# Gated mix of cached attention and a ReLU layer: part of w1 loaded as a separate 96-row transfer, VectorE and ScalarE in loops over one unit

## The chip, the cores and the metric

The kernel runs on one core of a Trainium2 chip. The metric is the device time of one execution in microseconds, as the median of several runs. The core has five engines with queues of their own: PE (TensorE, matmuls), DVE (VectorE), ACT (ScalarE), POOL (GpSimd) and SP (SyncE, which here issues every DMA). They meet only through semaphores. Sixteen DMA engines carry what SP issues.

## The reference

Batch is 2 with one token each (decode), D is 448, there are 16 heads of 256 and 4096 cached positions, and Dff is 1792. All arrays are float32.

```python
g = sigmoid((x * gate_w).sum(-1, keepdims=True))
q = (x @ wq), as 16 heads of 256
p = softmax(q . k_cache * 256**-0.5)          # over 4096 positions, for each of 2 x 16 heads
a = (p . v_cache), heads side by side, @ wo
b = relu(x @ w1) @ w2
out = g * a + (1 - g) * b
```

The caches are 268 MB of the 289.5 MB that are read.

## The kernel before, in words

**Units.** The work of the caches is cut into U = 32 units, one for each pair of batch and head. A unit's k and v are one block of 128 partitions x 16,384 floats (8.39 MB): the first half is k, the second v. Three such blocks fit in SBUF, slot[0] to slot[2]; unit u lies in slot (u + 1) mod 3. The first transfer, wq (with x and the gate's weights as its last 12 columns), takes slot[0]; kv[0] and kv[1] follow in slots 1 and 2.

**SP** (L170 to L192) issues all transfers in one queue. It refills a slot when the semaphore freed says that the unit in it is done: kv[u + 3] after unit u. The last unit's k and v halves come as two transfers (L181, L182), the second with a semaphore last_v of its own. Behind them, when unit 29 is done, come w1 and w2 into slot[0] (L184, L185), and, when unit 30 is done, wo into slot[1] in six pieces of 14, 8, 4, 3, 2 and 1 blocks of 448 columns (L189). The result goes out at L192.

**The start.** DVE spreads x over several columns (xr, xn and xl, L344 to L348), and PE computes the gate (L206) and q in two halves (project, L103 to L114; the transposes of q at L221). ACT copies them to SBUF (L309, L311).

**A unit** takes four steps. PE multiplies k with the query (L129, 16 matmuls that write sc in PSUM) and sets scored. DVE takes the negative maximum (L143) and sets maxed. ACT makes p = exp(sc + nm) with its sum (L136), sets raised, and copies the next unit's query to qc (L138, queried). DVE multiplies v with p in eight instructions that each sum up one column of ov (L149), and sets freed. PE can begin the next unit's scores as soon as the exp is through. DVE and ACT run ten passes of a loop over three units (L357, L316) and then two more units written out (L322, L363), with fixed addresses. PE loops over three units (L223).

**The tail.** PE starts the hidden layer h = x @ w1 when w1 has landed (L241, hidden). The 1792 columns are four groups of 448, one for each 32-row strip g of PSUM; the 448 rows of w1 are contracted in blocks of 128, 128, 128 and 64, the last of which holds two groups side by side in 128 partitions (L112). When freed reaches 32, PE transposes the maxima and sums (L244, L245), DVE and ACT work out the weights of the softmax's parts (L367 to L373), DVE scales ov into os (L375), and oc spreads the result (L378). ACT makes the ReLU (L326) and hr (L328, L331); PE multiplies hr with w2 (L267), and then oc with each piece of wo as it lands: 26 blocks into acc (L279), copied out by DVE (L382), and folded together with the last six blocks straight into z (L287, L292). DVE copies z to res (L384), and SP sends it out.

Of the kernel before, what the change touches and what calls it, by code (L numbers as in the profile page):

```python
# [3 lines left out]
F32 = mybir.dt.float32  # L4
# [14 lines left out]
def gated_mix_decode(nc, wq, kv, wm, wo, out):  # L19
# [11 lines left out]
    NW = wq.shape[1] - KC * (B + 1)  # L31
    FG = 448
    NF = 14
    W1 = 2 * (2 * KF * FG + FG)
# [15 lines left out]
    slot = [nc.alloc_sbuf_tensor_at(f"slot{i}", [P, SW], F32, offset=first + i * SW * 4).ap() for i in range(SLOTS)]  # L50
# [13 lines left out]
    scored, maxed, raised, queried, freed = (ev() for _ in range(5))  # L64
# [11 lines left out]
    xn = sb("xn", P, P // B, B)  # L76
    ge = sb("ge", P, 1)
# [3 lines left out]
    qt = sb("qt", P, U, T)  # L81
# [3 lines left out]
    ov = sb("ov", P, U, J)  # L85
    p = sb("p", P, SG)
# [29 lines left out]
    xg = slot[0][:, NW:wq.shape[1]].rearrange("p (c b) -> p c b", c=KC)  # L116

    ident_0, ident_ok, par_ok, xl_0 = ev(), ev(), ev(), ev()
# [15 lines left out]
    def unit_act(u, u_wait, s, s_next, last=False):  # L134
        act.wait_ge(maxed, u_wait)
        act.activation(p, sc, AF.Exp, bias=nm[:, bass.ds(u, 1)], accum_out=ls[:, bass.ds(u, 1)]).then_inc(raised, 1)  # L136
        if not last:
            act.activation(qc[:, s_next, :], qt[:, bass.ds(u + 1, 1), :].rearrange("p o t -> p (o t)"),  # L138
                           AF.Copy).then_inc(queried, 1)

    def unit_dve(u, u_wait, s, v_sem=None):
        dve.wait_ge(scored, u_wait)
        dve.tensor_reduce(nm[:, bass.ds(u, 1)], sc, axis=AX.X, op=ALU.max, negate=True).then_inc(maxed, 1)  # L143
        dve.wait_ge(raised, u_wait)
        if v_sem is not None:
            dve.wait_ge(v_sem, 16)
        for j in range(J):
            v = slot[s][:, SW // 2 + j * SG:SW // 2 + (j + 1) * SG]
            m = dve.scalar_tensor_tensor(v, v, 1.0, p, op0=ALU.mult, op1=ALU.mult,  # L149
                                         accum_out=ov[:, bass.ds(u, 1), j].rearrange("p o -> p o"))  # L150
        m.then_inc(freed, 1)
# [4 lines left out]
    U1 = (LOOP - 1) * SLOTS  # L156

# [4 lines left out]
    w2 = slot[0][:, W1:W1 + NF * D]  # L162
    w_o = slot[1]

    with nc.Block(no_gpsimd_drain=True) as block:

        @block.sync
        def _(_e):
# [15 lines left out]
            sp.dma_start(w1, wm[:, :W1]).then_inc(w1_in, 16)  # L184
            sp.dma_start(w2, wm[:, W1:]).then_inc(w2_in, 16)  # L185
# [49 lines left out]
        def pe_tail():  # L235
            half = W1 // 2
            def hidden(lo, hi):
                return project(pa, w1, lambda c, g: g // 2 * half + (g % 2 * KF + c) * FG,
                               lambda i: i * half + 2 * KF * FG, FG, lo, hi)

            pe.wait_ge(w1_in, 16)  # L241
# [8 lines left out]
            hidden(KF, KC).then_inc(hid_mm, 1)  # L250
            pe.wait_ge(os_ok, 1)
# [52 lines left out]
        def _(_e):  # L304
            act.wait_ge(gate_mm, 1)
# [139 lines left out]
```

## Time and profile before

| what | value |
|---|---|
| time, median of 3 runs | 676.09 us (675.98 to 676.59) |
| the profiled execution | 675.9 us |
| its span, first to last instruction | 674.5 us |
| read from HBM | 289.54 MB, 429 GB/s over the span |
| busy | PE 215.3 us, DVE 340.9 us, ACT 46.4 us, POOL 0.8 us |
| granted TensorE clock, mean | 0.674 |

The span is 1.4 us shorter than the execution's own time. Times in the views count from the span's start. The busy shares add up over the span and say nothing of what waits for what. A timeline row has its start, its length, the engine, the line, what was written and read, and in brackets the idle time before it with what ended it. A row of the windows view has the stretch, its length, each engine's busy time with the number of instructions, the granted clock, the mean busy share of the 16 DMA engines, and GB/s. A DMA share below 1 means that some of the sixteen have nothing to carry.

### The profile page before, as it was taken

What the parts mean: (1) busy time and instruction counts of PE and PEld (TensorE: products, weight loads), DVE (VectorE), ACT (ScalarE), POOL (GpSimd) and SP (SyncE); (2) the same over time, 40 slices, a digit from 0 to 9 for tenths busy, and PEclk for the clock granted to TensorE, in tenths of its full rate; (3) what the DMA queues carried; (4) which work ended last, traced back from release to release, by engine and by line L of the source; (5) the groups of instructions that cost most, each with busy time, mean ns of one, the idle gap of its engine ahead of it and who ended that gap; (6) DMA issues with size and microseconds to landing.
All of it is one profiled execution on the core that took longest, in us unless ns stands there. A gap on an engine that the chain in (4) does not pass through costs nothing.

```text
span 674.5 us, 3929 instructions
## 1 busy us (share of the span) xinstructions
PE 215.3 (32%) x1279; PEld 52.6 (8%) x1279; DVE 340.9 (51%) x566; ACT 46.4 (7%) x107; POOL 0.8 (0%) x7
## 2 busy tenths in 40 slices
PE   0643212333232213323321233333212333332456
PEld 0210000000000000000000000000000000000012
DVE  0015566554555665454556645446566544556670
ACT  0010000000000000000000000000000000000110
POOL 0000000000000000000000000000000000000000
PEclk9976566676756677676556767765676776655878
DMA  9999999999999999999999999999999999999997
GB/s 381 428 435 436 436 435 435 435 435 435 435 435 435 435 435 435 435 435 431 435 435 435 435 435 435 435 435 435 435 435 435 435 435 431 435 435 408 432 431 301
DMA packets 6084, 289.61 MB, mean 429 GB/s; under 512 B 704, under 2 KB 832, under 8 KB 1216
## 3 DMA queue, kind: packets, MB, share of 16 engines
q1 hardware_dynamic: 6080, 289.55, 99.2%
q8 instruction: 3, 0.05, 0.0%
q14 instruction: 1, 0.01, 0.0%
HBM read 289.54 MB, written 0.01 MB: 429 GB/s over the span
## 4 chain that ended last, share of the span: by engine, by line
DMA 68%; DVE 13%; PE 12%; issue 6%; ACT 1%; DVEq 1%; SPq 0%; ACTq 0%
DMA slot<-in_kv 64%; DVE slot L149 11%; PE sc L129 10%; DMA slot<-in_wo 3%; DVE nm L143 2%; PE acc L279 1%; ACT p L136 1%; DVEq L149 1%; PE z L292 0%; SPq L176 0%; DVE a_sb L382 0%; DVEq L143 0%; ACTq L136 0%; PE z L287 0%; SPq L66 0%
## 5 line engine op out<-in xcount | busy, mean ns | idle before, releaser
L149 DVE SCALAR_TENSOR_TENSOR slot<-slot,p 128x1024 f32<-128x1024 f32 x256 | 295.9, 1222 | 47.1 <-ACT p L136 47.1
L129 PE MATMUL sc<-slot,qc 128*32 128x512 f32 x1024 | 182.9, 880 | 415.9 <-DMA slot<-in_kv 415.9
L143 DVE TENSOR_REDUCE nm<-sc 128x1024 f32 (+1 forms) x32 | 39.2, 1225 | 243.7 <-PE sc L129 243.7
L129 PEld LDWEIGHTS sc<-slot,qc 128*32 128x32 f32 x1024 | 41.3, 154 | 556.9 <-issue 552.6
L136 ACT ACTIVATE p<-sc,nm 128x1024 f32<-128x1024 f32 x32 | 35.7, 1114 | 562.9 <-DVE nm L143 562.9
L149 DVE DVE_READ_ACCUMULATOR slot<-slot,p (+1 forms) x256 | 21.5, 84 | 0.0
L344 DVE COPY xr<-slot 128x384 f32<-128x384 f32 x1 | 0.6, 553 | 18.1 <-DMA slot<-in_wq 18.1
L206 PE MATMUL pa<-slot,xr 128*128 128x1 f32 x6 | 1.4, 355 | 21.4 <-DVE xl L348 21.4
L279 PE MATMUL acc<-slot,oc 128*32 128x448 f32 x52 | 7.2, 672 | 3.2 <-DMA slot<-in_wo 3.2
L109 PE MATMUL pb<-slot,xr 128*32 128x512 f32 x48 | 8.1, 829 | 0.0
L382 DVE COPY a_sb<-acc 128x448 f32<-128x448 f32 x1 | 0.6, 625 | 14.6 <-PE acc L279 14.6
L109 PE MATMUL pa<-slot,xr 128*32 128x448 f32 x24 | 4.0, 793 | 12.1 <-DMA slot<-in_wm 12.1
L136 ACT ACTIVATION_READ_ACCUMULATOR p<-sc,nm (+1 forms) x32 | 6.2, 193 | 0.0
L138 ACT ACTIVATE qc<-qt 128x2 f32 (+1 forms) x31 | 6.0, 192 | 0.0
L267 PE MATMUL acc<-slot,hr 128*32 128x448 f32 x28 | 3.2, 541 | 1.0 <-ACT hr L331 1.0
L206 PEld LDWEIGHTS pa<-slot,xr 128*128 128x128 f32 x6 | 1.4, 325 | 21.4 <-DVE xl L348 21.4
L279 PEld LDWEIGHTS acc<-slot,oc 128*32 128x32 f32 x52 | 2.3, 126 | 8.2 <-issue 6.9
L112 PE MATMUL pb<-slot,xl 128*64 128x512 f32 x8 | 2.2, 618 | 0.0
L109 PEld LDWEIGHTS pb<-slot,xr 128*32 128x32 f32 x48 | 1.7, 137 | 4.0 <-issue 4.0
L109 PEld LDWEIGHTS pa<-slot,xr 128*32 128x32 f32 x24 | 0.8, 141 | 14.3 <-DMA slot<-in_wm 13.0
L309 ACT ACTIVATE q<-pb 128x512 f32<-128x512 f32 x2 | 1.2, 597 | 9.7 <-PE pb L112 9.7
L378 DVE COPY oc<-pc 128x256 f32<-128x256 f32 x4 | 1.4, 418 | 0.8 <-PE pc L254 0.8
(54 smaller groups left out, 21.0 us busy)
## 6 DMA issues: line engine op xcount, KB each, us to landing
slot<-in_kv SPq DMA_DIRECT2D x2, 4096.0 KB, 35.4
slot<-in_wq SPq DMA_DIRECT2D x1, 7174.0 KB, 19.6
slot<-in_wm SPq DMA_DIRECT2D x2, 3136.0 KB, 31.5
slot<-in_wo SPq DMA_DIRECT2D x1, 3136.0 KB, 23.6
slot<-in_wo SPq DMA_DIRECT2D x1, 1792.0 KB, 27.5
slot<-in_wo SPq DMA_DIRECT2D x1, 896.0 KB, 29.1
slot<-in_wo SPq DMA_DIRECT2D x1, 672.0 KB, 30.3
slot<-in_kv SPq DMA_DIRECT2D x31, 39.9
```

Source lines behind the costliest of these rows:

```text
L109: m = pe.matmul(dst[g * R:(g + 1) * R, :n], x_of(c), w[:, at(c, g):at(c, g) + n], start=(c == 0), stop=False)
L112: m = pe.matmul(dst[i * HP:(i + 1) * HP, :n], xl.rearrange("p j r b -> p (j r b)"), w[:, at_last(i):at_last(i) + n], start=False, stop=True)
L129: m = pe.matmul(sc[g * R:(g + 1) * R, c * CW:(c + 1) * CW], qc[:, s, t:t + 1].to_broadcast([P, R]), slot[s][:, lo:lo + CW], start=(t == 0) ...
L136: act.activation(p, sc, AF.Exp, bias=nm[:, bass.ds(u, 1)], accum_out=ls[:, bass.ds(u, 1)]).then_inc(raised, 1)
L138: act.activation(qc[:, s_next, :], qt[:, bass.ds(u + 1, 1), :].rearrange("p o t -> p (o t)"), AF.Copy).then_inc(queried, 1)
L143: dve.tensor_reduce(nm[:, bass.ds(u, 1)], sc, axis=AX.X, op=ALU.max, negate=True).then_inc(maxed, 1)
L149: m = dve.scalar_tensor_tensor(v, v, 1.0, p, op0=ALU.mult, op1=ALU.mult, accum_out=ov[:, bass.ds(u, 1), j].rearrange("p o -> p o"))
L206: m = pe.matmul(pa[:, :1], x_of(c, P) if c < KF else xn[r].rearrange("p r b -> p (r b)"), xg[r, c, B:], start=(c == 0), stop=(c == KC - 1))
L267: pe.matmul(acc[g * R:(g + 1) * R, :D], hr[:, k, :], w2[:, k * D:(k + 1) * D], start=(k < G), stop=False)
L279: m = pe.matmul(acc[g * R:(g + 1) * R, :D], o_of(k), w_o[:, k * D:(k + 1) * D], start=False, stop=(k >= n - G))
L309: act.activation(q, pb, AF.Copy, scale=SCALE).then_inc(q_ok, 1)
L378: m = dve.tensor_copy(oc[:, h], pc[:, h * B * J:(h + 1) * B * J].rearrange("p (o b j) -> p j o b", o=1, b=B) .to_broadcast([P, J, RB, B]))
```

## The change

**w1.** Two of the four groups of columns are contracted as before, in blocks of 128, 128, 128 and 64 rows. The other two are contracted in blocks of 128, 128, 96 and 96 rows. Their first two blocks stay in the array wm; the two of 96 rows form a new array, we, of 12 groups of 9 rows, of which the ninth is not used. SP loads w1's main part (128 x 4928), then we's 96 x 1792, then w2. PE waits for both parts of w1 (w1_in at 32), and has one matmul more. A third layout of x, xe, holds the 96 rows of x; it comes as three more columns of wq's array.

**Loops.** DVE and ACT run all 32 units in loops of one unit, with addresses computed from the loop's register; the three slots are one tensor, ring. DVE sums into a small tile on, which ACT copies to ov after each unit (waiting for freed). ACT copies a query in every pass, so that qt has a 33rd entry, which GpSimd sets to zero. DVE waits in every pass for last_v at 1, which GpSimd sets, and in the last at 17.

**Moved.** xr, xn, xl (and xe) are made by ACT, fold by GpSimd; PE waits for fold_ok ahead of L254's step.

```diff
-    W1 = 2 * (2 * KF * FG + FG)
+    PS = 96
+    W1 = 2 * KF * FG + FG + 4 * FG
+    WE = 4 * FG
...
-    slot = [nc.alloc_sbuf_tensor_at(f"slot{i}", [P, SW], F32, offset=first + i * SW * 4).ap() for i in range(SLOTS)]
+    ring = nc.alloc_sbuf_tensor_at("ring", [P, SLOTS * SW], F32, offset=first).ap()
+    slot = [ring[:, i * SW:(i + 1) * SW] for i in range(SLOTS)]
...
-    w2 = slot[0][:, W1:W1 + NF * D]
+    w1e = slot[0][:PS, W1:W1 + WE]
+    w2 = slot[0][:, W1 + WE:W1 + WE + NF * D]
...
             sp.dma_start(w1, wm[:, :W1]).then_inc(w1_in, 16)
+            sp.dma_start(w1e, we[:, :8]).then_inc(w1_in, 16)
             sp.dma_start(w2, wm[:, W1:]).then_inc(w2_in, 16)
...
+            pool.memset(qt[:, U, :], 0.0).then_inc(last_v, 1)
+            pool.wait_ge(par_ok, 1)
+            pool.tensor_scalar(fold, par[:, None, :].to_broadcast([P, RB, B]), 1.0 / RB, None, op0=ALU.mult
+                               ).then_inc(fold_ok, 1)
...
-            half = W1 // 2
+            half = 2 * KF * FG + FG
+
             def hidden(lo, hi):
-                return project(pa, w1, lambda c, g: g // 2 * half + (g % 2 * KF + c) * FG,
-                               lambda i: i * half + 2 * KF * FG, FG, lo, hi)
-
-            pe.wait_ge(w1_in, 16)
+                for c in range(lo, hi):
+                    for g in range(G):
+                        i, h = divmod(g, 2)
+                        if i == 0 and c == KF:
+                            if g == 0:
+                                pe.matmul(pa[:HP, :FG], xl.rearrange("p j r b -> p (j r b)"),
+                                          w1[:, 2 * KF * FG:half], start=False, stop=True)
+                            continue
+                        x, at = x_of(c) if c < KF else xe.rearrange("p r b -> p (r b)"), (h * KF + c) * FG
+                        if i:
+                            at = half + (h * 2 + c) * FG if c < 2 else (h * 2 + c - 2) * FG
+                        w = w1e if i and c >= 2 else w1
+                        m = pe.matmul(pa[g * R:(g + 1) * R, :FG], x[:PS] if w is w1e else x, w[:, at:at + FG],
+                                      start=(c == 0), stop=(c == KC - 1))
+                return m
+
+            pe.wait_ge(w1_in, 32)
...
+            pe.wait_ge(fold_ok, 1)
             pe.wait_ge(os_ok, 1)
...
+            act.wait_ge(slot_in[0], 16)
+            act.activation(xr, xg[:, :KF, None, :B].to_broadcast([P, KF, P // B, B]), AF.Copy)
+            act.activation(xn, xg[:, KF:KC, :B].to_broadcast([P, P // B, B]), AF.Copy)
+            act.activation(xe, xg[:, KC:, :B].to_broadcast([P, RB, B]), AF.Copy)
...
-            with nc.Fori(0, LOOP - 1, engines=(ET.Activation,)) as r:
-                u0 = act.snap(r * SLOTS)
-                for k in range(SLOTS):
-                    u = act.snap(u0 + k)
-                    unit_act(u, u + 1, (k + 1) % SLOTS, (k + 2) % SLOTS)
-            for u in range(U1, U):
-                unit_act(u, u + 1, (u + 1) % SLOTS, (u + 2) % SLOTS, u == U - 1)
+            qf = qc.rearrange("p s t -> p (s t)")
+            with nc.Fori(0, U, engines=(ET.Activation,)) as u:
+                act.wait_ge(maxed, u + 1)
+                act.activation(p, sc, AF.Exp, bias=nm[:, bass.ds(u, 1)], accum_out=ls[:, bass.ds(u, 1)]
+                               ).then_inc(raised, 1)
+                act.activation(qf[:, bass.ds((u + 2) % SLOTS * T, T)],
+                               qt[:, bass.ds(u + 1, 1), :].rearrange("p o t -> p (o t)"), AF.Copy).then_inc(queried, 1)
+                act.wait_ge(freed, u + 1)
+                act.activation(ov[:, bass.ds(u, 1), :].rearrange("p o j -> p (o j)"), on, AF.Copy).then_inc(kept, 1)
...
-            with nc.Fori(0, LOOP - 1, engines=(ET.DVE,)) as r:
-                u0 = dve.snap(r * SLOTS)
-                for k in range(SLOTS):
-                    u = dve.snap(u0 + k)
-                    unit_dve(u, u + 1, (k + 1) % SLOTS)
-            for u in range(U1, U):
-                unit_dve(u, u + 1, (u + 1) % SLOTS, last_v if u == U - 1 else None)
+            with nc.Fori(0, U, engines=(ET.DVE,)) as u:
+                v0 = dve.snap((u + 1) % SLOTS * SW)
+                dve.wait_ge(scored, u + 1)
+                dve.tensor_reduce(nm[:, bass.ds(u, 1)], sc, axis=AX.X, op=ALU.max, negate=True).then_inc(maxed, 1)
+                dve.wait_ge(raised, u + 1)
+                dve.wait_ge(last_v, (u + 1) // U * 16 + 1)
+                for j in range(J):
+                    v = ring[:, bass.ds(v0 + (SW // 2 + j * SG), SG)]
+                    m = dve.scalar_tensor_tensor(v, v, 1.0, p, op0=ALU.mult, op1=ALU.mult, accum_out=on[:, j:j + 1])
+                m.then_inc(freed, 1)
...
+    rest = w1[2 * P:, 1].reshape(2, PS, 2, FG).transpose(1, 2, 0, 3).reshape(PS // 8, 8, -1)
+    we = np.zeros((PS // 8, 9, rest.shape[2]), np.float32)
+    we[:, :8] = rest
+    w1 = np.concatenate([full, last, both], 1)
```

More of the change, by code (lines that the diff above doesn't have):

```diff
@@ L16, with gated_mix_decode @@
 DIRECT = (3, 2, 1)
-def gated_mix_decode(nc, wq, kv, wm, wo, out):
+def gated_mix_decode(nc, wq, kv, wm, we, wo, out):
     U, _, SW = kv.shape
@@ L63, in gated_mix_decode @@
     wo_in = [ev() for _ in ACC + DIRECT]
-    scored, maxed, raised, queried, freed = (ev() for _ in range(5))
+    scored, maxed, raised, queried, freed, kept = (ev() for _ in range(6))
     sp.dma_start(slot[0][:, :wq.shape[1]], wq).then_inc(slot_in[0], 16)
@@ L114, in project @@
         return m
-    xg = slot[0][:, NW:wq.shape[1]].rearrange("p (c b) -> p c b", c=KC)
-    ident_0, ident_ok, par_ok, xl_0 = ev(), ev(), ev(), ev()
+    xg = slot[0][:, NW:wq.shape[1]].rearrange("p (c b) -> p c b", c=KC + 1)
+    ident_0, ident_ok, par_ok, fold_ok, xl_0 = (ev() for _ in range(5))
     x_ok, gate_mm, gate_ok, ge_ok, gp_ok, omg_ok = (ev() for _ in range(6))
@@ L132, in unit_pe, with oc_of @@
         m.then_inc(scored, 1)
[L134 to L151, printed above, removed]
+    def oc_of(h):
+        return (pc[:, h * B * J:(h + 1) * B * J].rearrange("p (o b j) -> p j o b", o=1, b=B)
+                .to_broadcast([P, J, RB, B]))
     LOOP = -(-U // SLOTS)
     FULL = U - (LOOP - 1) * SLOTS
-    U1 = (LOOP - 1) * SLOTS
+    assert U == 32
     hid_mm, hid_ok, hid_tr, hr_ok = ev(), ev(), ev(), ev()
```

40 lines of the change are left out of this document (20 added, 20 removed).

## The prediction

> **What bounds the kernel now.** I read the page's queues and its chain first, then the windows view (busy time, granted clock and DMA share by stretch), then the timeline of both ends, and last the single lines that the change touches. From the page, the span, the queues (packets, MB, share of 16 engines) and the chain:
>
> ```profile
> span 674.5 us, 3929 instructions
> q1 hardware_dynamic: 6080, 289.55, 99.2%
> q8 instruction: 3, 0.05, 0.0%
> q14 instruction: 1, 0.01, 0.0%
> DMA 68%; DVE 13%; PE 12%; issue 6%; ACT 1%; DVEq 1%; SPq 0%; ACTq 0%
> ```
>
> The SP queue keeps the 16 DMA engines at work for 99.2% of the span, so bytes set the time. DVE and PE stand in the chain only because the view walks back through the wait for a free slot. The next rows show this, and how the transfers run out (the last two columns are the DMA share and GB/s):
>
> ```profile
> 100.00:600.00 500.00, 147.27 (x828) 33.06 (x820) 272.45 (x442) 33.73 (x78) 0.00 (x0) 0.64 1.00 434
> 669.60:671.40 1.80, 1.16 (x40) 0.93 (x44) 0.59 (x1) 0.00 (x0) 0.00 (x0) 1.00 0.27 106
> ```
>
> ```profile
> 669.60:669.80 0.20, 0.00 (x0) 0.00 (x0) 0.20 (x1) 0.00 (x0) 0.00 (x0) 1.00 0.86 332
> 669.80:670.00 0.20, 0.00 (x0) 0.00 (x0) 0.20 (x1) 0.00 (x0) 0.00 (x0) 1.00 0.52 197
> 670.00:670.20 0.20, 0.00 (x0) 0.00 (x0) 0.19 (x1) 0.00 (x0) 0.00 (x0) 1.00 0.28 108
> 670.20:670.40 0.20, 0.16 (x8) 0.16 (x12) 0.00 (x0) 0.00 (x0) 0.00 (x0) 1.00 0.20 81
> 670.40:670.60 0.20, 0.20 (x16) 0.20 (x12) 0.00 (x0) 0.00 (x0) 0.00 (x0) 1.00 0.18 72
> 670.60:670.80 0.20, 0.20 (x20) 0.20 (x12) 0.00 (x0) 0.00 (x0) 0.00 (x0) 1.00 0.12 45
> 670.80:671.00 0.20, 0.20 (x20) 0.17 (x8) 0.00 (x0) 0.00 (x0) 0.00 (x0) 1.00 0.14 54
> 671.00:671.20 0.20, 0.20 (x12) 0.00 (x1) 0.00 (x0) 0.00 (x0) 0.00 (x0) 1.00 0.12 45
> 671.20:671.40 0.20, 0.20 (x11) 0.20 (x12) 0.00 (x0) 0.00 (x0) 0.00 (x0) 1.00 0.05 18
> ```
>
> Over 500 us the share is 1.00 at 434 GB/s, 27.1 GB/s an engine. At the end the engines do not stop together. A share of 0.28 is 4.5 engines, 0.20 three, 0.12 two, 0.05 one. So about twelve have no more to do by 670.2, one more stops about 670.4, one about 670.6, and the last two about 671.3. The row of 1.8 us holds 0.27 x 1.8 = 0.49 us of work an engine: had all stopped together, it would have been at 670.1, some 1.2 us earlier. That is all that a better spread of bytes can win here.
>
> The timeline shows that the last landing sets the end:
>
> ```profile
> 655.87 3.20 PE L267 MATMUL acc<-slot,hr 128*32 128x448 f32 x28 [1.01 <-ACT hr L331]
> ...
> 662.25 7.25 PE L279 MATMUL acc<-slot,oc 128*32 128x448 f32 x52 [3.18 <-DMA slot<-in_wo]
> ...
> 672.51 0.59 SPq L192 DMA_DIRECT2D out<-res  x1
> ```
>
> PE has done everything else by 659.07 and then stands 3.18 us for the first piece of wo. From there each piece is used as it lands, and 3.2 us after the last (671.3 to 674.5) the span ends. So the tail's arithmetic has 3.2 us to spare, and the last engine's last byte has none.
>
> **The transfer in two pieces.** This is the term that decides. The DMA issues (KB each, us to landing) and the pieces in the program's order on SP, before and then after, from the last half of v to the first piece of wo:
>
> ```profile
> slot<-in_wm SPq DMA_DIRECT2D x2, 3136.0 KB, 31.5
> ...
> slot<-in_kv SPq DMA_DIRECT2D x31, 39.9
> ```
>
> ```order
> L182 DMA slot_51<-in_kv 128x8192
> L184 DMA slot_49<-in_wm 128x6272
> L185 DMA slot_49<-in_wm 128x6272
> L189 DMA slot_50<-in_wo 128x6272
> L189 DMA slot_50<-in_wo 128x3584
> ```
>
> ```order
> L172 DMA ring<-in_kv 128x8192
> L174 DMA ring<-in_wm 128x4928
> L175 DMA ring<-in_we 96x1x1792
> L176 DMA ring<-in_wm 128x6272
> L180 DMA ring<-in_wo 128x6272
> L180 DMA ring<-in_wo 128x3584
> ```
>
> The bytes stay: 128 x 4928 + 96 x 1792 elements are the 128 x 6272 of before. The new transfer is 688 KB, and its source has three levels (12 groups of 8 rows, a ninth row skipped), which before has nowhere. If it is spread over all 16 engines, each carries 43.0 KB of it and the term is nothing. If by its 12 groups, twelve engines carry 57.3 KB, 14.3 KB more: 14.3 / 27.1 = 0.53 us later; the other four carry none: 43.0 / 27.1 = 1.59 us earlier. Everything behind it on the queue (w2, wo) shifts engine by engine by as much. I take the twelve, since nothing but the skipped row stands between this source and a plain block of 96 rows. [...] No row here shows a transfer of that kind.
>
> What that is worth depends on which four. If they hold the last two engines and the third latest, those now stop by 671.3 - 1.59 = 669.7, and the end goes to the fourth latest (about 670.3) or the bulk's end (670.15), plus 0.53: 670.7 to 670.85. That is 0.45 to 0.6 us before 671.3; I take **-0.5 us**. If one of the last two is among the twelve, the end is 671.3 + 0.53: **+0.5 us**.
>
> **The loops.** DVE after the last pass and the turn of its loop, before (the last two units written out) and after (all 32 in the loop; ISA rows compute register addresses):
>
> ```order
> L149 SCALAR_TENSOR_TENSOR slot_49,ov<-slot_49,p 128x1024
> L357 REGISTER_ALU
> L357 COMPARE_AND_BRANCH
> L143 TENSOR_REDUCE nm<-sc 128x1
> L149 SCALAR_TENSOR_TENSOR slot_50,ov<-slot_50,p 128x1024 x8
> L143 TENSOR_REDUCE nm<-sc 128x1
> L149 SCALAR_TENSOR_TENSOR slot_51,ov<-slot_51,p 128x1024 x8
> L367 TENSOR_REDUCE nb<-pc 32x1
> ```
>
> ```order
> L376 ISA
> L376 SCALAR_TENSOR_TENSOR ring,on<-ring,p 128x1024
> L368 REGISTER_ALU
> L368 COMPARE_AND_BRANCH
> L381 TENSOR_REDUCE nb<-pc 32x1
> ```
>
> So units 30 and 31 now pay register work, a branch lies between them, and one lies ahead of nb. Their prices, from the line views (ns min/median/max) and the timeline, the first product in the loop (unit 29) and written out (unit 30), with DVE's idle time before it in brackets:
>
> ```profile
> L357 DVEq COMPARE_BRANCH  x10: 50/56/67, 90.3 to 612.2; - x10
> ```
>
> ```profile
> 609.67 1.23 DVE L149 SCALAR_TENSOR_TENSOR slot<-slot,p 128x1024 f32<-128x1024 f32 x1 [1.48 <-ACT p L136]
> ...
> 629.25 1.23 DVE L149 SCALAR_TENSOR_TENSOR slot<-slot,p 128x1024 f32<-128x1024 f32 x1 [1.27 <-ACT p L136]
> ```
>
> In the loop DVE stands 1.48 us between reduce and first product, while ACT makes the exp; written out it stands 1.27: 0.2 us for the register work of both engines. With one ISA more for the wait on the last v, and one ahead of the reduce, I take 0.3 us a unit, 0.6 for two, and 0.2 for two turns of the loop. ACT now waits for freed behind each exp, then copies on into ov; queued behind it is the next exp, which cannot start before DVE's reduce. The copy is like that of qc:
>
> ```profile
> L138 ACT ACTIVATE qc<-qt x31: 191/192/194, 49.0 to 629.1; 128x2 f32 x30, 128x2 f32<-128x2 f32 x1
> ```
>
> Its 0.2 us lie beside the reduce of 1.2 us: nothing. The projection has one matmul more:
>
> ```profile
> 652.23 0.97 PE L112 MATMUL pa<-slot,xl 128*64 128x448 f32 x4
> ```
>
> Two matmuls of four passes took 0.97 us, so +0.5. PE's wait for w1_in now covers both pieces, so that its first half may start 0.53 us late; it has to be through when DVE frees unit 31:
>
> ```profile
> 647.01 3.05 PE L109 MATMUL pa<-slot,xr 128*32 128x448 f32 x16 [12.09 <-DMA slot<-in_wm]
> ...
> 650.23 0.28 PE L244 MATMUL pc<-ident,nm 128*32 128x128 f32 x1 [0.17 <-DVE slot L149]
> ```
>
> It ended at 650.06, so that 0.4 us would show, if DVE did not itself come 0.8 us later (above): nothing more. Sum on the tail's arithmetic: 0.6 + 0.2 + 0.5 = 1.3 us, under the 3.18 us for which PE waits for wo (2.7 if wo comes 0.5 earlier). Nothing shows; without that cover it would be +1.3. In the 30 units before, freed comes 0.3 us later; a slot's transfer takes 39.9 us from issue to landing, of which 8.39 MB at 434 GB/s are 19.3, so 20 us of queue hide it. [...]
>
> **The start.** xr, xn and xl go from DVE to ACT, with xe added, and fold to GpSimd, which is idle until then:
>
> ```profile
> 20.41 0.55 DVE L344 COPY xr<-slot 128x384 f32<-128x384 f32 x1 [18.13 <-DMA slot<-in_wq]
> ...
> 29.70 0.60 ACT L309 ACTIVATE q<-pb 128x512 f32<-128x512 f32 x1 [6.13 <-PE pb L112]
> ...
> 36.35 0.20 ACT L315 ACTIVATE qc<-qt 128x2 f32<-128x2 f32 x1
> ...
> 39.83 6.48 PE L129 MATMUL sc<-slot,qc 128*32 128x512 f32 x32 [3.75 <-DMA slot<-in_kv]
> ```
>
> ACT copies 512 columns in 0.60 us, DVE 384 in 0.55: about the same, plus 0.2 for xe and some 0.2 for a fixed cost in each. The query is ready at 36.55, PE then waits until 39.83 for kv[0], so 0.4 us is hidden. wq grows from 57,392 to 57,404 bytes a row, no longer a multiple of 16; nothing before has such a row. At the same rate it is 1.5 KB in all, nothing; at half rate 17 us. I take nothing.
>
> **The sum.** 674.5 - 0.5 = 674.0 us of span; the profiled execution took 675.9, so 675.4. The median of the runs is 676.09: **675.6 us**.
>
> **The rivals.** About 0.2%, 1.35 us, can be told from no change.
> 1. *A late engine is among the twelve* (0.36): +0.5, 676.6 us. For it: nothing in the page says which engines are late; four drawn at random would hold both of the last two once in twenty. Against: the late ones are about four, apart from a bulk of twelve, and the page has four instruction fetches in the span, whose packets run on these engines, which would single out the same few. [...]
> 2. *The small transfer runs on 8 engines or fewer* (0.06): on 8 each carries 86.0 KB, 1.59 us more. With a late one among them the end is 677.7 us, slower by 0.24%; 9 engines would be 1.2 us, so 8 is where it decides. For it: no transfer of before has such a source. Against: 12 divides into it evenly.
> 3. *The tail's arithmetic comes late* (0.04): if a turn of the loop cost 2 us more than the branch row says, twice on the path, 1.3 + 4.0 - 2.7 = +2.6, 678.2 us. The 67 ns speak against it.
> 4. *wq's row slows its transfer* (0.03): up to +17 us.
> 5. *Nothing moves* (0.06): the transfer is spread over all 16: 676.1 us.
>
> **How the numbers follow.** The forecast has 0.45. It and the fifth are within 0.2%; so is the first, its scatter (the runs span 0.6 us) aside. Levelling wins at most 1.2 us, so faster by over 0.2% needs that scatter: 0.06. Slower: 0.09, from the second (where a late one is in it), third and fourth, and the first's edge. Same: 0.85. The range: 0.7 below the forecast for the most of levelling, and up to 677.0 for the first with its scatter.
>
> **What would show it.** In the windows after: a share that stays near 0.75 for about 1 us or less before the end (four engines done), then falls quickly, is the forecast; a share of 0.05 to 0.12 lasting until 671.8 is the first rival. w2's and wo's landings, PE's wait ahead of the first acc<-wo matmul (above 1 us, or the third rival), and the first use of wq (at 20.41 before) show the rest. A change of over 1.35 us either way would make it wrong.

## The result, and the profile after

| | before | after |
|---|---|---|
| median | 676.08 us (675.86 to 677.01, 6 runs) | 680.25 us (678.6 to 681.19, 6 runs) |
| ratio of the runs | | 1.0054, 95% interval 1.0043 to 1.0065 |
| profiled execution, its span | 675.9 us, 674.5 us | 678.6 us, 676.3 us |

The changed kernel is slower by 0.54%, and the forecast's range (674.9 to 677.0) does not hold the time. The profiled execution is the mildest of the six: their spans are 676.3, 678.0, 678.5, 678.8, 678.5 and 677.6 us. So the profile shows 1.8 us of span, where the middle of the runs has some 3.7. What lies outside the span is 2.3 us in it, 1.6 to 2.7 in the six, and 1.4 in the profiled execution of before.

The page after, span, queues and chain:

```profile
span 676.3 us, 4179 instructions
q1 hardware_dynamic: 6188, 289.56, 99.4%
q8 instruction: 2, 0.03, 0.0%
DMA 70%; DVE 12%; PE 9%; issue 6%; DVEq 1%; ACT 1%; SPq 0%; ACTq 0%
```

The bytes are the same and the 16 engines are as busy as before (99.4%, 99.2% before). The loss is therefore not idle engines. It is engines that are busy and move less, as the windows below show. (Two of before's four instruction fetches are gone, 0.03 MB in all.)

The timeline after, from the last unit's first score matmul on:

```profile
620.40 1.03 SPq L175 DMA_DIRECT2D ring<-in_we  x1
...
630.33 5.34 PE L134 MATMUL sc<-ring,qc 128*32 128x512 f32 x32 [4.50 <-DMA ring<-in_kv]
...
649.52 3.21 PE L246 MATMUL pa<-ring,xr 128*32 128x448 f32 x16 [13.86 <-DMA ring<-in_we]
...
659.54 3.20 PE L277 MATMUL acc<-ring,hr 128*32 128x448 f32 x28 [1.01 <-ACT hr L352]
...
664.16 3.20 PE L289 MATMUL acc<-ring,oc 128*32 128x448 f32 x28 [1.43 <-DMA ring<-in_wo]
...
674.43 0.63 SPq L183 DMA_DIRECT2D out<-res  x1
```

and the same first row of before:

```profile
629.95 4.98 PE L129 MATMUL sc<-slot,qc 128*32 128x512 f32 x32 [3.27 <-DMA slot<-in_kv]
```

The last unit's scores are a good mark to count from, since everything up to there is alike (0.38 us apart, and the run with the loops alone, below, has 0.96). From that mark to the first matmul on w1 it was 17.06 us before and is 19.19 after, **2.13 us more**. To the issue of the result it was 42.56 and is 44.10, **1.54 us more**. What PE waits for at 649.52 is the new transfer, in_we.

The windows view says why (the last three columns are granted clock, DMA share and GB/s). Before, the 5 us in which w1's last rows land, and 10 us behind:

```profile
645.00:650.00 5.00, 2.99 (x16) 0.59 (x16) 5.00 (x9) 0.00 (x0) 0.00 (x0) 0.52 1.03 442
652.00:662.00 10.00, 5.57 (x49) 2.15 (x49) 1.84 (x5) 1.45 (x4) 0.00 (x0) 1.00 0.97 413
```

After:

```profile
645.00:650.00 5.00, 0.48 (x4) 0.20 (x8) 5.00 (x9) 0.00 (x0) 0.00 (x0) 0.50 0.99 283
652.00:662.00 10.00, 8.37 (x63) 2.82 (x61) 2.63 (x10) 1.70 (x5) 0.00 (x0) 0.88 0.96 415
```

With a share of 0.99 the engines moved 283 GB/s where they had moved 442. In these 5 us 0.8 MB less went through, 1.8 us at 434 GB/s. From 652 on the rate is that of before (415 and 413). The end of the transfers after:

```profile
670.80:671.40 0.60, 0.60 (x8) 0.00 (x0) 0.00 (x0) 0.00 (x0) 0.00 (x0) 1.00 0.82 332
671.40:672.00 0.60, 0.00 (x0) 0.00 (x0) 0.54 (x1) 0.00 (x0) 0.00 (x0) 1.00 0.88 358
672.00:672.60 0.60, 0.46 (x20) 0.46 (x24) 0.09 (x1) 0.00 (x0) 0.00 (x0) 1.00 0.78 305
672.60:673.20 0.60, 0.60 (x28) 0.36 (x20) 0.00 (x0) 0.00 (x0) 0.00 (x0) 1.00 0.29 108
673.20:673.80 0.60, 0.60 (x22) 0.40 (x24) 0.00 (x0) 0.00 (x0) 0.00 (x0) 1.00 0.01 3
```

This is close to the picture that the forecast asked for: a share near 0.8 (two to four engines done), and then a quick fall instead of before's long tail of one or two. Only it lasts two microseconds and not one, and it lies at 673 and not at 671.

The trace also has a record of each row that an engine carries. In the piece of wo whose rows are as long (7168 bytes, 128 partitions) each took 272 ns, before and after. The 96 rows of the new transfer took 459 ns in the mean: 21 of them about 272, 53 of the other 75 from 500 to 570. The last record of wo ends 1.51 us later behind the mark than before, and the result comes 1.54 us later, so in this execution the landing still sets the end.

### The profile page after: what moved, and what is told of

It is laid out like the page before. It is cut to its first block, busy times and chain, and to the rows that moved or that the text cites. A ratio compares the mean times of both kernels' runs of the same rounds, so it can differ in the third digit from the quotient of the medians.

```text
span 676.3 us, 4179 instructions
## 1 busy us (share of the span) xinstructions
PE 213.1 (32%) x1281; PEld 52.1 (8%) x1281; DVE 339.8 (50%) x561; ACT 54.3 (8%) x145; POOL 1.1 (0%) x9
## 3 DMA queue, kind: packets, MB, share of 16 engines
q1 hardware_dynamic: 6188, 289.56, 99.4%
## 4 chain that ended last, share of the span: by engine, by line
DMA 70%; DVE 12%; PE 9%; issue 6%; DVEq 1%; ACT 1%; SPq 0%; ACTq 0%
DMA ring<-in_kv 65%; DVE ring L376 10%; PE sc L134 9%; DMA ring<-in_wo 5%; DVE nm L371 2%; DVEq L376 1%; ACT p L338 1%; PE z L302 0%; DVEq L368 0%; DVEq L373 0%; PE acc L289 0%; SPq L180 0%; SPq L166 0%; DVEq L371 0%; DVE a_sb L395 0%
## 5 line engine op out<-in xcount | busy, mean ns | idle before, releaser
L376 DVE SCALAR_TENSOR_TENSOR ring<-ring,p 128x1024 f32 x256 | 295.9, 1221 | 54.8 <-ACT p L338 54.8
L134 PE MATMUL sc<-ring,qc 128*32 128x512 f32 x1024 | 181.5, 874 | 419.0 <-DMA ring<-in_kv 419.0
L371 DVE TENSOR_REDUCE nm<-sc 128x1024 f32 x32 | 39.2, 1225 | 235.9 <-PE sc L134 235.9
L134 PEld LDWEIGHTS sc<-ring,qc 128*32 128x32 f32 x1024 | 41.1, 153 | 558.7 <-issue 558.7
L343 ACT ACTIVATE ov<-on 128x8 f32 x32 | 6.7, 208 | 309.0 <-DVE ring L376 309.0
L376 DVE DVE_READ_ACCUMULATOR ring<-ring,p 128x1 f32 x256 | 21.2, 83 | 0.0
L114 PE MATMUL pb<-ring,xr 128*32 128x512 f32 x48 | 7.0, 726 | 0.0
L289 PE MATMUL acc<-ring,oc 128*32 128x448 f32 x52 | 5.9, 544 | 2.8 <-DMA ring<-in_wo 2.8
L338 ACT ACTIVATION_READ_ACCUMULATOR p<-sc,nm x32 | 6.2, 193 | 0.0
L340 ACT ACTIVATE qc<-qt x32 | 6.2, 192 | 0.0
```

What stands on the lines that cost most here:

```text
L114: m = pe.matmul(dst[g * R:(g + 1) * R, :n], x_of(c), w[:, at(c, g):at(c, g) + n], start=(c == 0), stop=False)
L134: m = pe.matmul(sc[g * R:(g + 1) * R, c * CW:(c + 1) * CW], qc[:, s, t:t + 1].to_broadcast([P, R]), slot[s][:, lo:lo + CW], start=(t == 0) ...
L289: m = pe.matmul(acc[g * R:(g + 1) * R, :D], o_of(k), w_o[:, k * D:(k + 1) * D], start=False, stop=(k >= n - G))
L340: act.activation(qf[:, bass.ds((u + 2) % SLOTS * T, T)], qt[:, bass.ds(u + 1, 1), :].rearrange("p o t -> p (o t)"), AF.Copy).then_inc(quer ...
L343: act.activation(ov[:, bass.ds(u, 1), :].rearrange("p o j -> p (o j)"), on, AF.Copy).then_inc(kept, 1)
```

## The experiments

Theory A is that the 96 rows land at about half speed (459 ns a row in the mean against 272), because several engines write to the same part of SBUF at a time; if so, another place can give another rate. Rival B is the loops, rival C that it is a separate, small transfer, and rival D that twelve engines carry it, unevenly. T (the tail's arithmetic comes late) came up on the way. From e13 on the expectations call PE's clock theory C. Ratios are to the kernel before in the same session, with 95% intervals. "To w1" and "to the result" count from the last unit's first score matmul of the profiled run (before: 17.06 and 42.56 us).

| run | median us | ratio | to w1 | to the result |
|---|---|---|---|---|
| e1 loops only | 676.69 | 1.0001 (0.9991 to 1.001) | 17.07 | 42.34 |
| e2 96 rows only | 679.64 | 1.005 (1.0033 to 1.0067) | 20.08 | 44.96 |
| e3 128 rows | 677.12 | 1.0012 (1.0002 to 1.0021) | 17.64 | 43.29 |
| e4 rows 9 apart | 678.61 | 1.0036 (1.0023 to 1.0049) | 18.39 | 43.56 |
| e5 48 rows at 32 | 676.64 | 1.0006 (0.9997 to 1.0016) | 16.98 | 42.28 |
| e6 48 rows at 0 | 679.13 | 1.0042 (1.0028 to 1.0056) | 18.92 | 46.62 |
| e7 16 engines | 679.18 | 1.0051 (1.0034 to 1.0067) | 18.98 | 44.25 |
| e8 loaded twice | 681.5 | 1.0077 (1.006 to 1.0094) | 23.19 | 48.12 |
| e9 the change again | 679.08 | 1.0044 (1.0029 to 1.006) | 18.98 | 43.89 |
| e10 two waits | 679.5 | 1.004 (1.0029 to 1.0052) | 16.68 | 44.40 |
| e11 48 rows, two waits | 679.8 | 1.0046 (1.0033 to 1.0059) | 15.48 | 44.90 |
| e12 the same, no loops | 677.32 | 1.0017 (1.0006 to 1.0029) | 15.49 | 42.36 |
| e13 the change, filler | 679.27 | 1.0035 (1.0023 to 1.0047) | 18.71 | 43.71 |
| e14 before, filler | 675.97 | 0.9992 (0.9984 to 1.0001) | 17.07 | 42.62 |
| e15 e11, filler | 677.36 | 1.0011 (1.0002 to 1.002) | 15.50 | 43.79 |
| e16 e12, filler | 676.63 | 1.0002 (0.9993 to 1.0011) | 15.49 | 42.35 |
| e17 the change, filler at w1 | 679.45 | 1.0042 (1.0028 to 1.0056) | 18.65 | 44.50 |
| e18 e12, filler at w1 | 676.6 | 1.0001 (0.9992 to 1.001) | 15.49 | 42.33 |

### The two halves of the change

e1 is the changed kernel with w1 loaded and contracted as before:

```diff
-            sp.dma_start(w1e, we[:, :8]).then_inc(w1_in, 16)
...
-            pe.wait_ge(w1_in, 32)
+            pe.wait_ge(w1_in, 16)
```

> The changed kernel with w1 as before (one transfer of 128 x 6272, blocks of 128, 128, 128 and 64); loops, moved copies and the longer rows of wq stay. Theory A (the loss of 4 us is the separate 96-row transfer, whose rows land at half speed because engines write to the same part of SBUF at the same moment): the time of before, 676.1 us within 0.7, and PE's first matmul on w1 near 647.0 as before instead of 649.5. Theory B (the loops and the waits they add make the tail late): about 680 us, with PE's wait ahead of the first wo matmul gone.

e2 is the kernel before with the 96-row transfer and its matmuls alone:

```diff
+            sp.dma_start(w1e, we[:, :8]).then_inc(w1_in, 16)
...
-            pe.wait_ge(w1_in, 16)
+            pe.wait_ge(w1_in, 32)
```

> The kernel before with only the separate 96-row transfer and the matmuls that go with it; VectorE and ScalarE as before. Theory A: 679 to 680.5 us, PE's first matmul on w1 some 2.5 us later than before (near 649.5). Theory B: 676 us.

The loops alone give 676.69 us, a ratio of 1.0001, and their timeline has w1's first matmul 17.07 us behind the mark:

```profile
630.91 5.34 PE L132 MATMUL sc<-ring,qc 128*32 128x512 f32 x32 [4.59 <-DMA ring<-in_kv]
...
647.98 3.22 PE L112 MATMUL pa<-ring,xr 128*32 128x448 f32 x16 [11.72 <-DMA ring<-in_wm]
```

The transfer alone gives 679.64 us and 1.005, which is the change's own ratio. B is out: the whole loss is the transfer's.

### Whole rows, and eight transfers

e3 loads 128 rows (32 of zeros, which nothing reads), so that all 16 engines would carry 57.3 KB each:

```diff
-            sp.dma_start(w1e, we[:, :8]).then_inc(w1_in, 16)
+            sp.dma_start(slot[0][:, W1:W1 + WE], we).then_inc(w1_in, 16)
...
-    we = np.zeros((PS // 8, 9, rest.shape[2]), np.float32)
-    we[:, :8] = rest
+    we = np.zeros((P, rest.shape[1]), np.float32)
+    we[:PS] = rest
```

> The changed kernel, but the separate transfer has 128 whole rows (32 of them zeros that nothing reads), so all 16 engines carry 57.3 KB of it, as much as the twelve did. [...] Theory C (the small separate transfer itself is what costs, by its short rows or by one more landing to wait for): 679 us or more.

It moves a third more bytes in this transfer than the change, is as separate, and still costs only 0.8 us by the medians (676.34 before in its session), w1 coming 0.58 us later. That is the arithmetic of 14.3 KB an engine at 27.1 GB/s, 0.53 us, and its 128 rows took 272 ns each: C is out, and the forecast's rate holds for a transfer over all 128 partitions.

e4 cuts the 96 rows into eight transfers of 12 rows, 9 partitions apart, so that twelve engines would write to different parts:

```diff
-            sp.dma_start(w1e, we[:, :8]).then_inc(w1_in, 16)
+            for i in range(8):
+                sp.dma_start(slot[0][i:i + 100:9, W1:W1 + WE], we[i]).then_inc(w1_in, 16)
```

> The changed kernel, but the 96 rows go by eight transfers of 12 rows each, to partitions 9 apart (K is 108 with 12 rows of zeros in x), so that twelve engines still carry 57.3 KB each and four none, and the twelve rows under way at one time lie in different groups of partitions. Theory A: no collision, the transfer takes 8 x 272 ns on the twelve, and if the late engines are among the four idle ones the end comes 0.3 to 0.6 us before that of before: 675.5 to 675.9 us. If uneven load on twelve engines is what costs (theory D), 679 us or more. If the late ones are among the twelve, 676.6.

678.61 us lies between the theories. What this run computes is wrong, so its rows cannot be taken to have landed 9 apart, and it says nothing on places. With eight transfers in place of one it also changes two things at a time. It is inconclusive.

### The same bytes in another place

e5 cuts the same 192 half-rows into four blocks of 48 rows, side by side, on partitions 32 to 79. The source has twelve groups of 57.3 KB, as in the change, and PE has four matmuls more:

```diff
-    PS = 96
+    PS = 80
-    WE = 4 * FG
+    WE = 8 * FG
...
+    w1f = slot[0][32:PS, W1:W1 + WE]
...
-            sp.dma_start(w1e, we[:, :8]).then_inc(w1_in, 16)
+            sp.dma_start(w1f, we[:, :4]).then_inc(w1_in, 16)
```

> The changed kernel, but the 192 rows of the second half go as four blocks of 48 rows, side by side in one transfer to partitions 32 to 79 (12 groups of 4 rows, so again twelve engines with 57.3 KB each, and four with none; four matmuls more). [...] Theory D (twelve engines with more than the others cost by themselves): 679 us or more.

e6 is e5 with the same block on partitions 0 to 47; the products follow it there, and nothing else changes:

```diff
-    PS = 80
+    PS = 48
...
-    w1f = slot[0][32:PS, W1:W1 + WE]
+    w1f = slot[0][:PS, W1:W1 + WE]
```

> The same as the run with 48 rows at partitions 32 to 79, but at partitions 0 to 47: the same bytes, rows, engines and matmuls, only other places in SBUF. [...] Theory D: no difference between the two.

676.64 against 679.13 us. The timeline of e5, then of e6:

```profile
630.45 6.59 PE L134 MATMUL sc<-ring,qc 128*32 128x512 f32 x32 [3.36 <-DMA ring<-in_kv]
...
647.43 3.00 PE L250 MATMUL pa<-ring,xr 128*32 128x448 f32 x16 [10.40 <-DMA ring<-in_we]
...
672.73 0.62 SPq L184 DMA_DIRECT2D out<-res  x1
```

```profile
630.37 5.34 PE L134 MATMUL sc<-ring,qc 128*32 128x512 f32 x32 [4.26 <-DMA ring<-in_kv]
...
649.29 3.21 PE L250 MATMUL pa<-ring,xr 128*32 128x448 f32 x16 [13.59 <-DMA ring<-in_we]
...
676.99 0.63 SPq L184 DMA_DIRECT2D out<-res  x1
```

and their windows, e5 first:

```profile
645.00:650.00 5.00, 2.56 (x16) 0.60 (x16) 5.00 (x9) 0.00 (x0) 0.00 (x0) 0.50 0.96 413
652.00:662.00 10.00, 8.36 (x68) 3.11 (x67) 2.63 (x10) 1.70 (x5) 0.00 (x0) 1.00 1.01 430
```

```profile
645.00:650.00 5.00, 0.71 (x4) 0.20 (x8) 5.00 (x9) 0.00 (x0) 0.00 (x0) 0.50 0.94 252
652.00:662.00 10.00, 8.51 (x45) 2.29 (x42) 2.63 (x10) 1.70 (x5) 0.00 (x0) 0.84 1.03 398
672.60:675.60 3.00, 1.93 (x40) 0.89 (x40) 0.62 (x1) 0.00 (x0) 0.00 (x0) 1.00 0.83 322
```

Around the same transfer, of the same bytes in the same groups, 413 GB/s move with the block at one place and 252 at the other, with the engines equally busy (shares of 0.96 and 0.94). The records of the rows agree: all 48 took 535 ns in e5, as rows of 14,336 bytes over 128 partitions do, while in e6 11 of the 48 did and most others took twice as long (946 ns in the mean). D expected no difference between the two; the rates decide for A as far as the place goes. The runs do not overlap either: 675.77 to 677.27 us in e5, 678.72 to 680.46 in e6. The second row of e6 shows one thing more: its engines are still slower 4 us and more behind the transfer (398 GB/s at a share of 1.03, where e5 has 430 at 1.01), and at 672.6 to 675.6 they are still at work, when e5 was done. This profile is of the longest of e6's five executions, 680.46 us, so its 46.62 us to the result shows a larger loss than the median has.

By the records of the rows 75 of 96 were slow in the change, 37 of 48 in e6 and none of 48 in e5. Which engine writes which partition is in no row here, so that engines meet in the same part of SBUF, A's cause, is argued and not shown. What is shown is that the rate goes with the place.

### Sixteen engines, and twice the work

e7 leaves out the ninth row, so that the source is plain:

```diff
-            sp.dma_start(w1e, we[:, :8]).then_inc(w1_in, 16)
+            sp.dma_start(w1e, we).then_inc(w1_in, 16)
...
-    rest = w1[2 * P:, 1].reshape(2, PS, 2, FG).transpose(1, 2, 0, 3).reshape(PS // 8, 8, -1)
-    we = np.zeros((PS // 8, 9, rest.shape[2]), np.float32)
-    we[:, :8] = rest
+    we = w1[2 * P:, 1].reshape(2, PS, 2, FG).transpose(1, 2, 0, 3).reshape(PS, -1)
```

> The changed kernel without the ninth row of each group, so that the source is a plain block of 96 rows and all 16 engines take six rows (43.0 KB) each. [...] Theory C (a small separate transfer costs by itself): 679 us or more. If spreading over all 16 were all that matters: 676.1.

e8 loads the 96 rows a second time, to a place that nothing reads:

```diff
+    w1d = slot[0][:PS, W1 + WE + NF * D:W1 + 2 * WE + NF * D]
...
             sp.dma_start(w1e, we[:, :8]).then_inc(w1_in, 16)
+            sp.dma_start(w1d, we[:, :8]).then_inc(w1_in, 16)
...
-            pe.wait_ge(w1_in, 32)
+            pe.wait_ge(w1_in, 48)
```

> The changed kernel with the separate transfer issued twice, the second time to columns that nothing reads, so the suspected cost is doubled. [...] At the full rate of 272 ns a row it would be +2.2: 682.4. If only the wait for one more landing cost: 681 to 682.

In e7 the ratio is 1.0051, and w1 comes 1.9 us late. No row names its engines, but the end of its transfers fits sixteen: in the five stretches in which the change had shares of 0.82 to 0.01 it has 1.00, 0.80, 0.14, 0.12 and 0.02, a tail of about two engines as before, and the picture of four idle ones is gone. The 96 rows took 392 ns in the mean. D is out. Loaded twice, w1 comes 23.19 us behind the mark, 4.0 us later than in the change, and the result too. The rows took 486 ns in the mean, so eight of them on an engine 3.9 us. The bytes alone, 688 KB at 434 GB/s, would take 1.6. By the medians the second transfer adds less: e8 is 5.4 us above before, the change 4.2 (2.7 in e9, below).

Theory A's direction held in e5 and e6, where w1 comes 16.98 and 18.92 us behind the mark. e7's 679.18 us is what C's expectation covers, but e3 and e5 exclude C. e8's 681.5 was the expectation for a mere wait for one more landing (681 to 682); w1's 4.0 us and the slow rows speak against that. So the place is shown as the cause between e5 and e6, and how much a row loses in a given place is not worked out.

### Is it the landing, or the arithmetic behind it?

The runs of the changed kernel spread over 2.6 us, those of before over 1.2, and PE's cover ahead of wo had shrunk from 3.18 to 1.43 us. So the rest of the loss could be arithmetic that comes late. e9 is the changed kernel once more. e10 gives the 96 rows a semaphore of their own, so that PE may begin on w1's main part, and e11 does the same to e5; e12 is e11 without the loops:

```diff
-            sp.dma_start(w1e, we[:, :8]).then_inc(w1_in, 16)
+            sp.dma_start(w1e, we[:, :8]).then_inc(we_in, 16)
...
-            pe.wait_ge(w1_in, 32)
+            pe.wait_ge(w1_in, 16)
...
+            pe.wait_ge(we_in, 16)
             hidden(2, KF)
```

> The changed kernel once more, unaltered, so that its median stands beside those of the other three in one session. Both theories: 680.3 us, ratio 1.004 to 1.0065.

> The changed kernel with a semaphore of its own for the 96 rows: PE waits for w1's main part ahead of the first half of the hidden layer, and for the 96 rows only ahead of the second. The transfers are the same. Theory A (the loss is that the last bytes land later, since the transfer of 96 rows is slow): as the kernel of the change, 680 us, ratio 1.005, with PE's wait ahead of the first piece of wo back at 2 us or more. Rival T (the later landing of w1 counts because it starts the tail's arithmetic late, until that sets the end): 677.8 us or less, ratio 1.0025 or below. For both, the first matmul on w1 comes within 17.8 us of the last unit's first score matmul, and not 19.2.

> The changed kernel with four blocks of 48 rows side by side on partitions 32 to 79 (twelve engines with 57.3 KB each, as in the change), and a semaphore of its own for them. Theory A: no engine waits for another in this transfer, and the four idle engines hold the late ones, so that the end comes as the forecast had it: 675.4 to 676.0 us, ratio 0.999. Rival T: with 48 rows alone the tail's arithmetic was just as late as the last landing, so the second wait wins 0.5 us or more against 676.64: 676.1 us or less. Against both: 676.6 us again would say that neither wait nor level counts any more.

> The kernel before, with DVE and ACT written as there, and only w1's transfer changed: the 48 rows side by side on partitions 32 to 79, with two waits. Theory A: the forecast's levelling without the loops' 0.6 us in the tail: 675.4 to 675.9 us, ratio 0.999. Rival T: the same as the run with loops within 0.3 us where the tail's arithmetic is covered, 0.5 us better where it is not.

e10 began on w1 2.3 us earlier behind the mark than e9 and won nothing (679.5 against 679.08): what T expected misses. What A expected beside it, PE's wait ahead of wo back at 2 us, did not come either, since PE's granted clock was 0.50 from 652.0 to 666.6. With the arithmetic slow again e10 does not settle T; e17, below, says more. e12 gives 677.32 us in three groups, where 675.4 to 675.9 were expected. e11 is the surprise. It has e5's transfers and begins on w1 1.5 us earlier than e5, and yet takes 679.8 us where e5 takes 676.64 (ratios 1.0046 and 1.0006). Neither theory had that. Its windows:

```profile
645.40:648.60 3.20, 3.17 (x16) 0.60 (x16) 3.20 (x7) 0.00 (x0) 0.00 (x0) 0.50 1.09 468
648.60:652.00 3.40, 1.40 (x16) 0.52 (x14) 2.52 (x9) 0.46 (x2) 0.00 (x0) 1.00 0.92 398
652.00:665.60 13.60, 12.05 (x52) 3.71 (x52) 2.10 (x6) 1.44 (x4) 0.00 (x0) 0.50 0.99 424
...
670.00:671.00 1.00, 1.00 (x12) 0.35 (x6) 0.00 (x0) 0.00 (x0) 0.00 (x0) 1.00 0.26 99
671.00:672.00 1.00, 1.00 (x8) 0.17 (x4) 0.00 (x0) 0.00 (x0) 0.00 (x0) 1.00 0.00 0
```

and the row of its timeline between the first two:

```profile
650.65 0.28 PE L257 MATMUL pc<-ident,nm 128*32 128x128 f32 x1 [2.00 <-DVE ring L381]
```

The transfers were through before 671, earlier than before's 671.3. But PE, having begun early, stood idle for 2.0 us until DVE was done; its granted clock fell to 0.5 at 652.0 and stayed there for 13.6 us, in which matmuls took about twice as long (the two on xl 1.75 us, where e5 has 0.97). At the end PE no longer waited for any transfer. So in e11 PE at the low clock sets the end. That the idle time of the earlier start brought the fall is argued here, and e15 below bears it out.

In the 3.40 us ahead of the fall PE was busy for 1.40 us at a clock of 1.00; in the 13.60 us at 0.50 it was busy for 12.05. What lets the clock fall, and what brings it back at 665.6, is not shown.

### Filler matmuls

Does the clock also cost the changed kernel its loss? Matmuls that nobody reads, on PE where it waits, keep it busy (e13: the change; e14: before; e15: e11; e16: e12):

```diff
+        def warm(n):
+            for _ in range(n):
+                pe.matmul(z[:, :KF * P], ident, xr.rearrange("p c r b -> p (c r b)"), start=True, stop=True)
...
+            warm(18)
             pe.wait_ge(w1_in, 32)
...
+            warm(4)
             pe.wait_ge(oc_ok, 1)
```

> The changed kernel, with 18 matmuls whose result nobody reads put on PE between the last unit's scores and its wait for w1, and 4 ahead of its wait for oc, so that PE is not idle there. The transfers are the same. Theory A alone (what is lost is when the last bytes land): as the changed kernel, 679 to 680.3 us, runs spread over 3 us as before. Theory C (the landing is 1 to 1.6 us late, and the rest of the loss is the tail's arithmetic at a granted clock of 0.5 in some runs): clock 1.0 through the tail in the profile, the slow end of the runs gone, median 677.3 to 678.4 us, ratio 1.002 to 1.003.

> The kernel before with the same filler (15 matmuls ahead of the wait for w1, 2 behind its first half, 4 ahead of the wait for oc). Both theories: the end of before is set by the last landing with the arithmetic 3.2 us ahead, so a faster PE wins nothing: 676.0 to 676.5 us, ratio 1.000 within 0.001. Should it come below 675.6, the arithmetic counted in before, too.

> The run with 48 rows on partitions 32 to 79 and two waits (679.8 us), with the filler (13, 4 and 4 matmuls). Theory A alone cannot say why that run was slow, since its transfers ended early. Theory C: clock 1.0 from the first matmul on w1 on, the arithmetic early again, and the end set by the last landing, that is where the forecast put it: 675.4 to 676.2 us, ratio 0.998 to 1.000, runs within 1.5 us.

> The run with 48 rows, two waits and no loops (677.32 us, in three groups of 676.2, 678.1 and 679.7), with the filler (13, 3 and 4). Theory C: only the group at 676.2 is left, or better: 675.4 to 676.3 us, ratio 0.998 to 1.000. If the three groups remain, they are not the clock's.

e15 takes back 2.4 us (679.8 to 677.36; e5 has 676.64), and the three groups of e12 (676.03 to 679.77 us) become one (675.65 to 677.04, e16). From 645.4 to 648.6 and from 652.0 to 665.6 the granted clock is 1.00 and 0.87 in e15's profile, where it was 0.50 both times in e11's. So PE's idle time, and by these profiles the clock, is what spread those; no execution of e12's later groups was profiled. Both medians are above what was expected (675.4 to 676.2 and 675.4 to 676.3). Before stays (0.9992, interval to 1.0001), as an end that hangs on the landing must. But the changed kernel stays too: 679.27 us, where the clock's theory had 677.3 to 678.4. It missed by a microsecond.

In e15 the filler ahead of oc was itself in the way: the matmuls on the first three pieces of wo, 5.46 us without a wait, began only when it was through.

```profile
663.02 2.85 PE L234 MATMUL z<-xr,ident 128*128 128x384 f32 x8
665.80 5.46 PE L301 MATMUL acc<-ring,oc 128*32 128x448 f32 x52
```

So e17 and e18 drop those four, from e13 and e16:

```diff
-            warm(4)
             pe.wait_ge(oc_ok, 1)
```

> The changed kernel with the 18 filler matmuls ahead of the wait for w1 alone, and none ahead of the wait for oc. In the run with both, four of six runs were at 679.2 to 679.6 us. Theory C with the filler itself in the way (the 4 behind w2's matmuls lie ahead of the first piece of wo, 2.9 us at clock 1.0): that group goes, 677.3 to 678.0 us, ratio 1.0015 to 1.0025, which is the late landing alone. If the group at 679.3 stays, that part of the loss is not PE's start: either a fall of the clock later in the tail, or the landing itself later in some runs than in others.

> The kernel before with 48 rows on partitions 32 to 79 and two waits, with the filler of 13 and 3 matmuls around the first half of the hidden layer and none ahead of oc. Theory C: what the filler ahead of oc cost is saved, and the end is the last landing with four idle engines levelled in: 675.2 to 676.0 us, ratio 0.998 to 0.9995, faster than both kernels if the forecast's half microsecond is real. At 676.3 or above, the levelling wins nothing.

e17's timeline has PE through with w2 early and back at 3.20 us of wait, the full cover of before:

```profile
658.00 3.20 PE L282 MATMUL acc<-ring,hr 128*32 128x448 f32 x28 [1.01 <-ACT hr L357]
664.40 6.04 PE L294 MATMUL acc<-ring,oc 128*32 128x448 f32 x44 [3.20 <-DMA ring<-in_wo]
...
674.71 0.62 SPq L183 DMA_DIRECT2D out<-res  x1
```

and the kernel takes 679.45 us all the same (677.3 to 678.0 were expected, had the clock been it). In this execution the last record of wo ends 1.90 us later behind the mark than before, and the result comes 1.94 us later. The arithmetic is out as the cause of this part of the loss; the landing sets the end. e18, meant to beat both kernels, is at 676.6 us and does not. Two of its eleven runs are at 675.64 and 675.74, where the forecast's levelling would put them, and nine at 676.35 to 676.99; the profile is of the first, and why the nine are later is open.

**What stays open.** The profiled runs of the changed transfer have the result 1.2 to 2.4 us late (e9, e10, e13, e17, e2); the medians are 2.7 to 4.2 us up. The missing one to two microseconds are in executions that were not profiled. One profile of a long execution there is, e6's at 680.46 us, and in it the transfers stay slower to the end; whether the change's longer ones do the same no run shows. Nor does any run show which engine wrote where.

## Why the prediction was wrong

**The step that failed** is the price of the transfer: "twelve engines carry 57.3 KB, 14.3 KB more: 14.3 / 27.1 = 0.53 us later". The bytes were right, as far as the shape of the end tells (below). The rate was not: 27.1 GB/s an engine was read from transfers over all 128 partitions, and taken for one over 96, and nothing in the trace of before spoke for it. A row took 459 ns in the mean, and 272 over 128 partitions. Eight such rows are 3.7 us on an engine, where six at 272 ns, the even share of 16 engines, are 1.6: about 2 us later by this estimate. Measured, w1 came 2.13 us late, not 0.53, and in e2 3.0, and the last landing 1.5 us late where the forecast had it half a microsecond early. In e5, where the place is free of the trouble, the rate holds (all 48 rows at 535 ns). There w1 is not even the 0.53 us late (16.98 against 17.06 us), and why is open. Behind the step lies an unknown that was bounded on one side only. The prediction bounded how many engines would carry the transfer (8, 12, 16), never how fast an engine is, although the row of we had no like in the trace of before.

**The four idle engines.** That twelve engines carry the transfer was the author's estimate, and no row names them. Right is the shape: the end (0.82, 0.88, 0.78, 0.29) shows engines done early, and in e7, whose end fits 16 engines, before's long tail is back. The half microsecond that this was to win is not shown. Where the place is free of the trouble, the last record of wo ends 41.13 (e5), 41.21 (e18) and 40.69 us (e11) behind the mark, against 41.44 before; but e1, with w1's transfer as before, has 41.23, and no median of these runs lies below before's.

**The tail's arithmetic.** The forecast's terms were 1.3 us of work under 2.7 us of cover, so that 1.4 would be left, and PE's wait is 1.43. That is chance. w2's matmuls come 3.3 us later behind the mark (29.21 against 25.92), of which 2.13 are the wait for both pieces; beside it stand one matmul more and a granted clock of 0.5 until 654.5 (before: 649.8). The forecast let the wait cost 0.53 us and no more. The wait for wo survives only because wo is 1.5 us late as well.

**The loops.** Nearly right, and e1 shows that they cost nothing. The rows of the turn, and of DVE's wait ahead of the last unit's first product, after:

```profile
L368 DVEq COMPARE_BRANCH  x32: 50/56/56, 50.9 to 643.5; - x32
```

```profile
641.05 1.23 DVE L376 SCALAR_TENSOR_TENSOR ring<-ring,p 128x1024 f32 x1 [1.71 <-ACT p L338]
```

A turn takes 56 ns, as taken from before; the last unit's register work costs 1.71 - 1.27 = 0.44 us where 0.3 was taken. No run shows the 2 us more a turn that the third rival assumed; all 32 took 50 to 56 ns.

**The start.** Right: ACT's first use of wq is at 20.39 us, against 20.41.

```profile
20.39 0.52 ACT L316 ACTIVATE xr<-ring 128x384 f32<-128x384 f32 x1 [18.38 <-DMA ring<-in_wq]
```

**The rivals.** None was the one. The first (a late engine among the twelve) is not borne out by the shape of the end; the second is refuted by the same shape (a share near 0.8, where eight engines would leave 0.5); the fourth by the start. The third came near the profiled execution's time (678.2 against 678.6) by a mechanism that did not happen: luck. The fifth's condition is that of e7, whose end fits all 16 engines, and its time is not 676.1 but 679.18 us. Slower came out as unlikely because every rival on the transfer was priced in bytes at one rate.

## What to carry to other kernels

In these runs the rate of a transfer depended on where it landed. The rate of the transfers over 128 partitions held for 48 rows on partitions 32 to 79 (535 ns a row), and not for 96 rows on 0 to 95 (459 ns in the mean against 272) or 48 on 0 to 47 (946 against 535). Where the new shape is not in the trace, the rate needs bounds as much as the bytes do. A DMA share of 0.99 went with 283 GB/s here, one of 1.03 with 442; look at GB/s beside the share, stretch by stretch. What told this loss apart was moving the same bytes to another place and changing nothing else (e5 to e6).

## What the runs showed of the hardware

- A transfer of 688 KB brings w1 on time on partitions 32 to 79 and 1.9 us late on 0 to 47, in the same twelve groups either time (413 and 252 GB/s in the same 5 us; 535 and 946 ns a row).
- Starting PE 1.5 us earlier made a kernel some 3 us slower (e5 to e11): in the profiled execution the granted clock fell to 0.5 for 13.6 us behind 2.0 us of idle time, and filler matmuls in the idle time won back 2.4 us (e15).
- SP takes 1.03 us to issue the 96-row transfer with its skipped rows, 0.43 for the same 96 rows from a plain source (e7), and 0.33 to 0.46 for the others of w1 and w2.
